# Seven half products in the last unit's output layer, TensorE transposes for the second unit, and a newly fitted order of steps

## The chip, the core and the metric

The kernel runs on one core of a Trainium2 chip. The metric is the device time in microseconds. A profiled execution was recorded as well: its trace gives the start and end of every instruction, and its "span" is the time from the first to the last of them.

## What is computed

The reference is a gated linear recurrence followed by a feed-forward block. The recurrence has 4 batches, 8 heads, 768 positions and a head size of 48.

```python
mag = np.sqrt(a_re * a_re + a_im * a_im)
scale = np.minimum(mag, 0.999) / (mag + 1e-06)
a_re_n, a_im_n = (a_re * scale, a_im * scale)
...
for t in range(S):
    new_re = ar * S_re - ai * S_im
    new_im = ar * S_im + ai * S_re
    S_re, S_im = (new_re + kv, new_im)          # kv: outer product of k[t] and v[t]
    y[:, :, t] = np.einsum('bhd,bhde->bhe', q[:, :, t], S_re)
...
h = x @ w_in                                    # x: y as 3072 x 384; w_in 384 x 2048
sp = np.maximum(h, 0.0) + np.log1p(np.exp(-np.abs(h)))
g = h * erf(sp)
return (g @ w_out).astype(np.float32)           # w_out 2048 x 384
```

## The kernel before

**Tiling.** The 3072 tokens are cut into 12 units of 256 tokens (three to a batch), each unit u into two chunks c of 128 tokens. The recurrence is done in chunks: running sums of the logarithms and angles of the gates, keys and queries scaled and turned by them, scores of a chunk with a triangular mask, and a state carried from chunk to chunk. The feed-forward block works on a whole unit: 2048 hidden columns in two slabs (`sl`) of 8 tiles, four steps of two tiles each.

**The order.** The Python program does not emit the work unit by unit. Every piece of work is a generator, called a step, and the string `ORDER` names the steps one after another; each mention advances that step to its next `yield` (the loop at the end of `quotient_path`). So the string fixes, word by word, the order in which each engine's in-order queue gets its instructions, and SyncE's (SP) queue its transfers. All instructions are there for the same work whatever the order; only the ACT table loads depend on it, since `act` (L780 to L786) emits one (L785) only where the next function belongs to another set than the last one (Ln and Exp; Arctan and Sin; Gelu). The names used below:

- `n0`..`n15` load a piece of the weights as 64-bit words and make float32 of it on VectorE (DVE, L843 to L848). `i0`..`i15` ("look") load a piece again and reduce it on DVE (L858). For i below 14 that load goes into the buffer that the slabs call `z` or `yy`, of which there is one each.
- `m t o l r a s p` with a unit number are the gates: ACT functions, DVE arithmetic, running sums on TensorE (PE).
- `k q v g` are loads. `K` and `Q` are `prep` (L1040, L1045): two DVE multiplications that write `kt` or `qt`. Keys and queries are then needed with the head dimension on the partitions, in a tile `KQ` (one buffer). **Unit 0** gets there by `kT` and `qT` (`turn`, L1069 and L1073): four PE transposes into PSUM and a copy out of it. **Units 1 to 11** get there by a DVE transpose of blocks (L1051, a third yield of `prep`) into a tile `X`, and by `M` (`move`, L1062): twelve transfers of 64 KB on SP's queue that put the blocks in their places.
- `A` are the scores (PE L1082, DVE L1086), `S` the state (PE L1101), `Y` the result (PE L1137, ACT copy L1139 into `xT`).
- `h` is `ff_in`: 6 matmuls (12 records in the trace, L1150) and an ACT copy (L1153); there are two PSUM buffers for it. `x` is `softplus`: four ACT functions over a whole slab, in the single buffers `z` and `yy`. `e` is `erf_times_h`: a Gelu on ACT into `e` (two buffers) and four DVE operations (L1178 to L1184), four parts to a slab. `z` is free for the next slab once its last L1180 has read it, `yy` once the last L1182 has.
- `O` is the output product. **Units 0 to 2 and unit 11** use `ff_out_8` (L1211): 16 steps of two matmuls with 384 columns (L1219), then an ACT scaling (L1226) and the store. **Units 3 to 10** use `ff_out_7` (L1241): the product is written as a 2x2 block product in half tiles, of which seven are computed instead of eight. Fourteen steps `O{u}.0` to `O{u}.13` of four matmuls with 192 columns each (L1254): a product for each slab, X, Y, Z and W being PSUM tiles. It needs sums of blocks of h: `f{u}.{sl}` (two DVE operations, L1195 and L1197), `sum_2` (L1265) once d (`O.1`, `O.2`) has read them, `read_x` (L1269) once b (`O.4`, `O.5`) has; and its PSUM tiles are brought out by DVE (L1262, L1274).
- The sums of the weights that the seven products use are made in place by `b0`..`b6` (L893), so the second half of `w_out_sb` in each first half slab is no longer there for unit 11. `d0` and `d1` (`restore`, L1238) put it back into a tile `B12`, and unit 11's `ff_out_8` takes two matmuls of 192 columns (L1221, L1222) for such a tile.
- `u` are matmuls whose result is not read. `Z` is `check`: DVE reductions, one PE product (L1326), DVE comparisons (L1330, L1331) whose result is read by all engines for a branch at the end.

Of the kernel before, what the change touches and what calls it, by code (L numbers as in the profile page):

```python
# [10 lines left out]
FP = mybir.dt.float32  # L11
# [9 lines left out]
P = 128  # L21
# [28 lines left out]
g0.0 u2_25 u2_41 u2_22 u4_2 u2_34 u4_38 u4_20 g0.0 u8_0 g0.1 g0.1 t0.0 m0.0 t0.0 t0.0 m0.0 m0.0 t0.1 l0.0 o0.0  # L50
t0.1 t0.1 l0.0 o0.1 l0.0 l0.0 l0.0 m0.1 m0.1 m0.1 l0.1 p0.0 p0.0 p0.0 u2_24 u8_1 n0 n0 n0 n0 n1 n1 n1 n1 r0.0
a0.0 n3 n3 a0.0 a0.0 a0.0 k0.0 u4_21 K0.0 n3 u2_23 r0.1 a0.1 a0.1 u2_40 q0.0 Q0.0 s0.0 s0.0 s0.0 K0.0 l0.1
kT0.0.1 Q0.0 qT0.0.0 qT0.0.1 a0.1 l0.1 l0.1 g1.0 t1.0 t1.0 qT0.0.0 a0.1 s0.1 l0.1 kT0.0.1 n3 g1.0 t1.0 v0.0 g1.1
t1.1 kT0.0.0 kT0.0.0 o1.0 p0.1 n2 n2 qT0.0.1 A0.0.1 A0.0.1 S0.0 g1.1 t1.1 p0.1 n2 p0.0 t1.1 k0.1 p0.1 K0.1 n2
r1.0 a1.0 a1.0 s0.1 s0.1 K0.1 m1.1 m1.1 m1.1 o1.1 v0.1 m1.0 a1.0 A0.0.0 p0.0 S0.0 a1.0 A0.0.0 n4 m1.0 m1.0 q0.1
Q0.1 n6 kT0.1.1 n4 p0.1 kT0.1.1 l1.1 l1.1 l1.0 l1.0 Q0.1 l1.1 S0.1 l1.0 l1.0 S0.1 l1.1 n4 Y0.0 kT0.1.0 kT0.1.0
l1.0 l1.1 n4 qT0.1.1 qT0.1.1 qT0.1.0 qT0.1.0 A0.1.1 A0.1.1 n5 p1.0 A0.1.0 A0.1.0 p0.1 S0.1 n5 q1.0 Y0.0 p1.0
Q1.0 p1.0 s1.0 s1.0 k1.0 K1.0 n5 r1.1 g2.1 s1.0 Q1.0 a1.1 K1.0 Q1.0 K1.0 Y0.1 Y0.1 p1.1 p1.1 a1.1 n5 a1.1 a1.1
q1.1 Q1.1 g2.0 m2 t2 t2 g2.0 g2.1 m2 h0.0.2 h0.0.2 m2 l2 l2 n6 s1.1 p1.1 t2 n6 l2 l2 o2 l2 n6 k1.1 h0.0.0 h0.0.0
p1.0 h0.0.4 v1.0 r2 n7 s1.1 s1.1 h0.0.6 h0.0.6 h0.0.4 x0.0 x0.0 e0.0.0 n7 l2 M1.0 M1.0 M1.0 M1.0 K1.1 l2 n7 Q1.1  # L60
n7 A1.0.0 A1.0.0 A1.0.1 A1.0.1 S1.0 n8 K1.1 a2.0 q2.0 p1.1 v1.1 k2.0 Q1.1 Y1.0 Y1.0 K1.1 p1.0 h0.1.6 n9 S1.0
M1.1 a2.0 M1.1 a2.0 a2.0 n8 e0.0.2 a2.0 a2.0 a2.0 a2.1 h0.1.6 p2.0 p2.0 p2.1 p2.1 p2.0 n8 n8 a2.1 n9 a2.1 a2.1
S1.0 Q2.0 h0.1.0 h0.1.0 p2.1 a2.1 a2.1 a2.1 s2 n9 n9 M1.1 M1.1 K2.0 S1.1 u2_39 A1.1.0 A1.1.0 A1.1.1 A1.1.1 g3.1
g3.0 s2 s2 K2.0 Q2.0 g3.0 S1.1 K2.0 g3.1 t3 t3 t3 m3 m3 p1.1 S1.1 o3 r3 Y1.1 Y1.1 a3.0 m3 l3 q2.1 h0.1.4 Q2.1
k2.1 Q2.0 h0.1.4 h0.1.2 v2.0 S2.0 p2.0 l3 h0.1.2 Q2.1 l3 K2.1 a3.0 a3.0 x0.0 K2.1 a3.0 x0.0 n10 n10 h1.1.0
h1.1.0 l3 h1.0.0 S2.0 l3 n10 l3 a3.0 l3 p3.0 p3.1 p3.1 p3.1 p2.0 p3.0 p3.0 h1.0.0 S2.0 h1.0.2 M2.0 M2.0 M2.0
e0.0.2 e0.0.0 M2.0 A2.0.1 A2.0.0 e0.0.2 e0.0.0 a3.1 a3.1 e0.0.2 e0.0.0 a3.1 a3.1 e0.0.0 e0.0.4 a3.1 A2.0.1
e0.0.2 a3.1 h1.0.2 e0.0.6 a3.1 s3 s3 s3 h1.0.6 g4.1 n11 g4.0 p3.0 g4.1 q3.0 h1.0.6 m4 k3.0 h1.0.4 h1.0.4 t4
A2.0.0 Y2.0 h1.1.6 K2.1 v2.1 g4.0 e0.0.4 t4 m4 n10 Q2.1 e0.0.4 e0.0.6 M2.1 M2.1 h1.1.2 e0.0.4 n11 e0.0.4 n11
e0.0.6 O0.1 Q3.0 K3.0 e0.0.6 m4 M2.1 M2.1 n12 p3.0 e0.0.6 K3.0 n11 x0.1 n13 v3.0 l4 x0.1 l4 l4 k3.1 t4 Q3.0 o4  # L70
l4 K3.0 l4 Y2.0 x0.1 O0.0 O0.2 O0.4 A2.1.1 A2.1.1 x0.1 l4 Q3.0 l4 a4.0 A2.1.0 A2.1.0 e0.1.0 e0.1.0 e0.1.2 e0.1.2
e0.1.0 e0.1.2 h1.1.6 e0.1.0 e0.1.2 e0.1.0 r4 a4.0 e0.1.2 e0.1.6 e0.1.6 a4.0 a4.0 O0.3 O0.5 O0.7 e0.1.4 e0.1.4
n12 Y2.1 Y2.1 e0.1.6 h1.1.4 h1.1.4 h1.1.2 e0.1.4 S3.0 n12 a4.0 a4.0 a4.0 q3.1 M3.0 M3.0 M3.0 n12 p3.1 M3.0
e0.1.6 e0.1.4 n13 K3.1 n13 S3.0 a4.1 a4.1 Q3.1 x1.0 x1.0 x1.0 a4.1 O0.6 h2.0.0 O0.8 O0.9 A3.0.0 n13 p4.0 p4.0
p4.1 p4.1 p4.1 p4.0 x1.0 h2.0.2 a4.1 K3.1 a4.1 O0.11 n15 v3.1 S3.1 O0.10 n15 e0.1.4 n15 e0.1.6 n15 e1.0.2 e1.0.2
e1.0.0 e1.0.0 e1.0.2 e1.0.0 e1.0.2 g5.1 e1.0.0 e1.0.2 e1.0.0 g5.0 g5.1 g5.0 p4.0 n14 h2.0.0 m5 a4.1 h2.0.2 m5 m5
n14 e1.0.6 e1.0.6 h2.0.6 h2.0.6 n14 e1.0.4 n14 e1.0.4 t5 e1.0.6 e1.0.4 e1.0.4 l5 Q3.1 t5 K3.1 e1.0.6 Q3.1 h2.1.0
h2.1.0 l5 x1.1 A3.0.1 A3.0.1 l5 l5 t5 l5 e1.0.4 x1.1 h2.1.2 h2.1.2 M3.1 M3.1 x1.1 M3.1 O0.12 O0.14 O0.13 O0.15
O0.15 h2.1.4 x1.1 h2.0.4 e1.0.6 a4.1 l5 A3.0.0 O1.0 O1.2 O1.4 o5 l5 e1.1.0 e1.1.0 e1.1.2 e1.1.2 e1.1.0 e1.1.0
e1.1.0 e1.1.2 s4 s4 r5 s4 e1.1.2 e1.1.2 q4.1 k4.0 K4.0 K4.0 e1.1.4 e1.1.4 e1.1.4 p3.1 M3.1 v4.1 e1.1.6 e1.1.6  # L80
h2.1.4 e1.1.6 e1.1.6 O1.6 Y3.0 O1.8 A3.1.1 A3.1.1 A3.1.0 A3.1.0 O0.15 v4.0 a5.0 q4.0 h2.1.6 O1.10 O0.14 O0.14
h2.0.4 x2.0 O1.1 S3.1 S3.1 Y3.1 Y3.0 S4.0 e1.1.4 x2.0 a5.0 a5.0 K4.0 k4.1 K4.1 x2.0 Q4.0 e1.1.4 Q4.0 Y3.1 Q4.0
e1.1.6 p4.1 M4.0 a5.0 K4.1 Q4.1 S4.0 x2.0 q5.1 M4.0 M4.0 M4.0 e2.0.0 e2.0.0 e2.0.0 h2.1.6 e2.0.2 e2.0.2 e2.0.0
e2.0.2 e2.0.0 e2.0.2 e2.0.2 O1.12 p5.0 p5.0 p5.0 h3.0.6 h3.0.6 O1.14 e2.0.6 e2.0.6 p5.1 O1.3 O1.5 a5.0 a5.0 a5.0
a5.1 e2.0.6 h3.0.2 e2.0.4 e2.0.4 e2.0.4 e2.0.4 O1.14 p5.1 p5.1 q5.0 x2.1 e2.0.4 a5.1 a5.1 e2.0.6 e2.0.6 x2.1
h3.0.2 x2.1 h3.0.0 h3.0.0 A4.0.0 O2.0 S4.1 Q4.1 a5.1 a5.1 A4.0.1 p4.0 S4.0 Q4.1 A4.0.0 S4.1 k5.0 O2.2 A4.0.1
Y4.0 v5.1 K5.0 K4.1 a5.1 a5.1 x2.1 e2.1.0 e2.1.0 e2.1.0 e2.1.2 e2.1.2 e2.1.2 e2.1.2 e2.1.0 s5 s5 e2.1.0 e2.1.2
s5 K5.0 p4.1 g6.0 g6.1 g6.1 e2.1.4 e2.1.4 O1.14 g6.0 e2.1.6 e2.1.6 e2.1.6 e2.1.6 e2.1.4 Y4.0 M4.1 v5.0 k5.1 S4.1
M4.1 M4.1 M4.1 m6 m6 h3.0.4 h3.0.4 x3.0 O1.7 O1.9 O1.11 O1.13 h3.1.4 O1.15 A4.1.1 S5.0 m6 l6 O1.15 t6 K5.0 Q5.0
Q5.0 Q5.0 l6 A4.1.0 A4.1.0 O2.1 x3.0 O2.3 A4.1.1 Y4.1 e2.1.4 l6 l6 e2.1.6 Q5.1 e2.1.4 Q5.1 v6.0 q6.0 l6 l6 x3.0  # L90
t6 t6 S5.0 h3.1.4 x3.0 o6 l6 K5.1 e3.0.2 e3.0.2 e3.0.0 e3.0.0 e3.0.2 e3.0.0 e3.0.2 e3.0.0 r6 e3.0.2 e3.0.0
h3.1.2 h3.1.2 a6.0 a6.0 e3.0.6 e3.0.6 O2.5 O2.7 O2.4 h3.1.6 e3.0.4 h3.1.6 e3.0.4 e3.0.6 e3.0.4 h3.1.0 h3.1.0
a6.0 a6.0 M5.0 a6.0 v6.1 M5.0 M5.0 M5.0 A5.0.0 a6.1 O1.15 p5.0 p5.0 A5.0.1 A5.0.1 A5.0.0 x3.1 O2.6 O2.9 O2.11
Y4.1 x3.1 Y5.0 e3.0.4 e3.0.6 K5.1 a6.1 a6.1 K5.1 x3.1 b6 a6.1 Q5.1 e3.0.6 M5.1 a6.1 a6.1 a6.1 b4 e3.0.4 Y5.0
f3.0 f3.0 x3.1 b0 S5.0 e3.1.2 e3.1.2 e3.1.0 s6 e3.1.2 e3.1.2 e3.1.0 e3.1.0 O2.13 e3.1.2 e3.1.0 e3.1.0 p6.1 p6.1
O2.8 p6.0 p6.0 Q6.0 e3.1.4 O2.15 h4.0.0 h4.0.0 e3.1.4 e3.1.4 e3.1.6 e3.1.6 e3.1.6 O2.10 O2.12 O2.14 g7.0 g7.1
g7.1 g7.0 M5.1 m7 M5.1 M5.1 m7 m7 b6 b2 e3.1.4 e3.1.6 e3.1.4 b4 b2 b0 b6 s6 s6 Q6.0 h4.0.2 h4.0.2 l7 O2.15 l7
h4.0.4 h4.0.4 i0 i0 h4.0.6 e3.1.6 f3.1 l7 h4.0.6 b0 b0 O2.14 l7 l7 k6.1 i1 x4.0 i1 t7 x4.0 t7 x4.0 p6.1 x4.0 b2
b2 b4 t7 A5.1.0 h4.1.6 O3.0 A5.1.0 A5.1.1 A5.1.1 l7 b4 l7 o7 p6.1 q6.1 O3.1 O3.2 O3.1 O3.2 e4.0.0 e4.0.0 e4.0.0
h4.1.6 e4.0.2 e4.0.2 e4.0.2 e4.0.0 e4.0.2 e4.0.0 e4.0.2 h4.1.0 h4.1.0 r7 b6 e4.0.6 e4.0.6 Y5.1 Y5.1 O3.3 e4.0.6  # L100
e4.0.4 e4.0.4 e4.0.4 Q6.0 f3.1 a7.0 e4.0.6 h4.1.4 h4.1.4 h4.1.2 h4.1.2 x4.1 O2.15 O2.14 e4.0.4 k6.0 p6.0 p6.0
p6.0 K6.0 a7.0 K6.0 O3.6 O3.4 O3.5 O3.5 O3.5 O3.4 O3.5 K6.0 M6.0 O3.7 h5.0.4 O3.7 e4.0.6 e4.0.4 M6.0 M6.0 x4.1
x4.1 a7.0 a7.0 Q6.1 O3.7 x4.1 K6.1 e4.1.2 e4.1.2 e4.1.0 e4.1.0 h5.0.2 e4.1.2 e4.1.0 e4.1.2 e4.1.2 p7.0 p7.0 p7.0
O3.8 a7.0 e4.1.0 e4.1.0 O3.9 O3.10 O3.11 O3.12 e4.1.6 e4.1.6 e4.1.6 h5.0.4 e4.1.4 e4.1.4 e4.1.4 e4.1.6 h5.0.2
a7.0 a7.0 e4.1.4 e4.1.4 p7.1 p7.1 M6.0 g8.0 p7.0 k7.0 f4.0 e4.1.6 i2 f4.1 a7.1 a7.1 O3.11 O3.13 O3.13 i2 a7.1
a7.1 f4.1 h5.0.0 h5.0.0 h5.0.6 h5.0.6 p7.1 x5.0 A6.0.0 A6.0.0 i3 i3 S6.0 S6.0 O4.1 O4.2 a7.1 a7.1 a7.1 O4.1 O4.2
p6.1 g8.1 x5.0 x5.0 O3.11 m8 O3.13 g8.0 g8.1 x5.0 Q6.1 Q6.1 f4.0 K6.1 K6.1 O4.0 O4.3 O4.4 A6.0.1 O4.5 O4.5
A6.0.1 O4.4 e5.0.0 e5.0.0 e5.0.0 e5.0.2 m8 m8 l8 e5.0.2 e5.0.0 e5.0.2 h5.1.4 h5.1.4 t8 l8 s7 l8 S6.1 e5.0.2
e5.0.0 e5.0.2 O4.5 l8 S6.1 O4.5 e5.0.4 e5.0.6 h5.1.0 h5.1.0 S6.1 l8 v7.1 p7.1 p7.0 M6.1 M6.1 q7.1 M6.1 M6.1
e5.0.4 e5.0.6 e5.0.4 O4.6 h5.1.2 O4.7 O4.7 e5.0.6 q7.0 K7.0 Q7.0 O4.7 e5.0.6 s7 s7 Q7.0 Y6.0 h5.1.2 K7.0 l8  # L110
e5.0.6 l8 e5.0.4 h5.1.6 h5.1.6 x5.1 t8 x5.1 Y6.0 x5.1 k7.1 v8.0 e5.0.4 A6.1.0 A6.1.0 t8 A6.1.1 A6.1.1 Q7.0 x5.1
K7.1 K7.0 O4.8 O4.9 O4.10 O4.11 v7.0 S7.0 e5.1.0 O4.12 Y6.1 Y6.1 S7.0 K7.1 o8 e5.1.0 e5.1.0 e5.1.2 e5.1.2 e5.1.0
# [569 lines left out]
def quotient_path(  # L682
# [27 lines left out]
    C = 2  # L710
# [722 lines left out]
```

## Time and profile before

| what | value |
|---|---|
| runs: median (lowest to highest of 3) | 674.85 us (671.51 to 676.1) |
| the profiled execution's own time | 671.15 us |
| its span | 669.4 us, 12235 instructions |
| last PE product of the output layer ends | 662.3 us |
| ACT table loads | 99, 127.0 us |
| `KQ` transfers | 264 of 64 KB |
| SP's queue, waiting for DVE's `X` | 76.1 us in 15 waits |
| mean granted PE clock | 0.996 |

In the profile, a group of instructions is given as line, engine, operation, "output<-input", then the count, the busy time in total and the mean of one in ns, and the engine's idle time just before. PE is TensorE's matmul, PEld its weight load, DVE VectorE, ACT ScalarE, SPq SyncE's queue of transfers. In the table by stretches each engine has its busy time and, in brackets, its number of instructions; then follow the clock granted to PE, the mean busy share of the 16 DMA engines and GB/s. In the timeline a row starts with start and length in us; the square bracket at the end is the idle time before it and what ended it.

### The profile page before, as it was taken

Reading aid. Unit: us, or ns where it says so; the run is one execution under the profiler, and the core shown is the slowest. Engines: PE = TensorE matmul, PEld = TensorE weight load, DVE = VectorE, ACT = ScalarE, POOL = GpSimd, SP = SyncE. Lnnn points to the kernel's source line nnn. Section 1 sums busy time; section 2 is a strip of 40 time slices with the busy share of each in tenths; the row PEclk is TensorE's granted clock in tenths of the full one; section 3 lists DMA queues with packets and bytes.
Section 4 is the critical chain, followed back from the end, with each engine's and each line's share of the span. In section 5 each row is a group of like instructions: output and inputs, shape, how many; then the busy total and the mean of one; then the engine's idle time right before and its main releaser. Section 6 shows DMA issues by size and latency. Waiting matters only on the chain.

```text
span 669.4 us, 12235 instructions
## 1 busy us (share of the span) xinstructions
PE 642.9 (96%) x4680; PEld 558.7 (83%) x4680; DVE 605.5 (90%) x984; ACT 581.5 (87%) x761; POOL 1.1 (0%) x8
## 2 busy tenths in 40 slices
PE   8788899999999999999999999999999999999995
PEld 7566787777677777999998999999998998999984
DVE  6999799999998999999999998999999898968844
ACT  6999889999999999996998997998998877676750
POOL 0000000000000000000000000000000000000000
PEclk9999899999999999999999999999999999999999
DMA  9877767762557328217526536625644534340000
GB/s 254 242 170 171 134 134 129 167 163 33 112 95 130 65 44 179 58 22 181 96 48 153 120 48 146 135 52 120 143 72 77 141 68 103 110 107 13 1 24 29
DMA packets 295468, 71.81 MB, mean 107 GB/s; under 512 B 282068, under 2 KB 285160, under 8 KB 295400
## 3 DMA queue, kind: packets, MB, share of 16 engines
q1 hardware_dynamic: 293320, 70.54, 49.5%
q8 instruction: 39, 0.64, 0.4%
q10 hardware_dynamic: 2080, 0.39, 0.3%
q14 instruction: 29, 0.24, 0.1%
HBM read 48.82 MB, written 4.75 MB: 80 GB/s over the span
## 4 chain that ended last, share of the span: by engine, by line
PE 39%; ACT 34%; DVE 16%; issue 4%; SPq 3%; DMA 3%; DVEq 0%; ACTq 0%
PE hps L1150 16%; ACT L785 7%; PE ops L1219 6%; ACT yy L786 6%; ACT z L786 5%; ACT CS L786 3%; PE sc L1082 3%; ACT e L786 3%; PE Z L1254 2%; PE X L1254 2%; SPq L1062 2%; PE y L1137 2%; DVE yy L1180 2%; ACT th L786 2%; DVE z L1178 2%
## 5 line engine op out<-in xcount | busy, mean ns | idle before, releaser
L1150 PE MATMUL hps<-xT,w_in_sb 128*128 128x256 f32 x1152 | 261.4, 381 | 1.5 <-ACT h L1153 1.3
L1150 PEld LDWEIGHTS hps<-xT,w_in_sb 128*128 128x128 f32 x1152 | 216.0, 190 | 34.5 <-ACT h L1153 4.3
L785 ACT ACT_TABLE_LOAD x99 | 127.0, 1283 | 3.7 <-issue 2.1
L1178 DVE TENSOR_TENSOR z<-z,yy 128x512 f32<-128x512 f32 x96 | 64.7, 687 | 23.0 <-ACT e L786 22.6
L786 ACT ACTIVATE e<-z 128x512 f32<-128x512 f32 x96 | 58.0, 628 | 22.8 <-DVE h L1184 22.2
L1219 PE MATMUL ops<-w_out_sb,h 128*128 128x384 f32 x224 | 77.3, 488 | 0.4 <-ACT out L1226 0.4
L1153 ACT COPY h<-hps 128x512 f32<-128x512 f32 x96 | 54.3, 577 | 14.8 <-PE hps L1150 14.8
L1180 DVE SCALAR_TENSOR_TENSOR yy<-z,yy 128x512 f32<-128x512 f32 x96 | 64.7, 688 | 1.7
L1184 DVE SCALAR_TENSOR_TENSOR h<-e,h 128x512 f32<-128x512 f32 x96 | 64.7, 685 | 1.2
L1182 DVE TENSOR_TENSOR e<-e,yy 128x512 f32<-128x512 f32 x96 | 64.6, 685 | 1.0
L1219 PEld LDWEIGHTS ops<-w_out_sb,h 128*128 128x128 f32 x224 | 41.6, 190 | 23.9 <-ACT out L1226 0.6
L1082 PEld LDWEIGHTS sc<-KQ 96*128 96x128 f32 x384 | 48.2, 194 | 9.7 <-issue 5.3
L1082 PE MATMUL sc<-KQ 96*128 96x128 f32 x384 | 50.3, 280 | 5.4 <-DMA KQ<-X 4.0
L786 ACT ACTIVATE z<-h 128x2048 f32<-128x2048 f32 x24 | 45.9, 1915 | 5.4 <-DVE seen L858 3.9
L786 ACT ACTIVATE yy<-z 128x2048 f32<-128x2048 f32 x24 | 45.9, 1913 | 2.1 <-DVE e L1182 1.8
L786 ACT ACTIVATE z<-z 128x2048 f32<-128x2048 f32 x24 | 45.8, 1910 | 0.4
L786 ACT ACTIVATE yy<-yy 128x2048 f32<-128x2048 f32 x24 | 45.9, 1914 | 0.3
L1086 DVE TENSOR_TENSOR A<-sc,triu 128x512 f32<-128x512 f32 x48 | 32.0, 681 | 3.4 <-PE sc L1082 3.4
L1137 PE MATMUL y<-A,v 128*32 128x128 f32 x768 | 33.7, 277 | 0.9 <-DVE A L1086 0.9
L1101 PEld LDWEIGHTS kv<-v,kt 128*96 128x96 f32 x320 | 29.7, 165 | 2.4 <-PE tr L1069 0.7
L1101 PE MATMUL kv<-v,kt 128*96 128x48 f32 x320 | 29.9, 246 | 0.5 <-PE tr L1069 0.5
L1137 PEld LDWEIGHTS y<-A,v 128*32 128x32 f32 x768 | 20.7, 110 | 8.0 <-issue 3.2
(119 smaller groups left out, 1043.2 us busy)
## 6 DMA issues: line engine op xcount, KB each, us to landing
KQ<-X SPq DMA_DIRECT2D x264, 64.0 KB
raw<-in_moe_w_in_dram SPq DMA_DIRECT2D x8, 768.0 KB
raw<-in_moe_w_out_dram SPq DMA_DIRECT2D x8, 768.0 KB
again<-in_moe_w_in_dram SPq DMA_DIRECT2D x8, 768.0 KB
ar<-in_a_re_dram SPq DMA_DIRECT2D x24, 192.0 KB
k<-in_k_dram SPq DMA_DIRECT2D x24, 192.0 KB
q<-in_q_dram SPq DMA_DIRECT2D x24, 192.0 KB
v<-in_v_dram SPq DMA_DIRECT2D x48, 96.0 KB
```

The lines of the kernel that those rows point to most:

```text
L785: scalar.preload_act_table_set(sets[0])
L786: scalar.activation(func=func, **kw)
L1082: nc.tensor.matmul(out=ps[:, j, :], lhsT=head("k", g * HG + j, u, c), rhs=head("q", g * HG + j, u, c), start=True, stop=True)
L1101: nc.tensor.matmul(out=kv[0:D2, j, :], lhsT=T["kt", u, c][:, j].rearrange("p u d -> p (u d)"), rhs=side(T["v", u][:, c, j // 2], j % 2), s ...
L1137: nc.tensor.matmul(out=ps[b * QUAD:(b + 1) * QUAD, i, :], lhsT=lhsT, rhs=rhs, start=start, stop=stop)
L1150: nc.tensor.matmul(out=ps[:, e, :], lhsT=w_in_sb[:, (sl * SLAB + i) // 2, kd, e * P:(e + 1) * P], rhs=T["xT", u][:, kd, :], start=(kd == 0 ...
L1153: scalar.copy(out=T["h", u, sl][:, i:i + 2, :], in_=ps)
L1178: vector.tensor_tensor(out=z, in0=z, in1=y, op=OP.mult)
L1180: vector.scalar_tensor_tensor(out=y, in0=z, scalar=-2.0, in1=y, op0=OP.add, op1=OP.mult)
L1182: vector.tensor_tensor(out=e, in0=e, in1=y, op=OP.mult)
L1184: vector.scalar_tensor_tensor(out=h, in0=e, scalar=1.0 / RT2, in1=h, op0=OP.add, op1=OP.mult)
L1219: nc.tensor.matmul(out=ps, lhsT=lhsT, rhs=w_out_sb[:, i, :], start=i == HALF, stop=i == KF - 1)
```

## The change

Three things are done.

1. `plain` loses `or u == NU - 1`: unit 11 uses `ff_out_7` and has `f11.0` and `f11.1`; `restore`, `B12`, `d0` and `d1` are gone.
2. `TURNS = 2`: units 0 and 1 use `turn`, units 2 to 11 `move`. In `turn` only the keys of unit 0's chunk 0 are copied by DVE, all others by ACT. `prep` of unit 1 has two yields.
3. `ORDER` is another string: 2303 words against 2291. Beside the words that 1 and 2 add and remove it has the same words, nearly all in other places. Read off the two strings, ACT changes its table set 99 times before and 94 times after.

`g_angle` takes the place of the previous chunk's angles later than before, in a function of its own; what it emits is the same.

```diff
+    TURNS = 2
...
-        prev = None
+        prev = lambda: T["F", u][:, c - 1, :] if c > 0 else T["F", u - 1][:, C - 1, :]
...
-        if u > 0:
+        if u >= TURNS:
             x = whole(att1, "X", (u, c), [P, D2 // QUAD, 2 * H, QUAD])
...
-        (vector.tensor_copy if nm == "k" and c == 0 else scalar.copy)(out=columns(u, c)[0:D2, i:i + HG], in_=ps[0:D2])
+        (vector.tensor_copy if nm == "k" and u == 0 and c == 0 else scalar.copy)(out=columns(u, c)[0:D2, i:i + HG], in_=ps[0:D2])
...
-                if u < PLAIN or e >= HALF:
-                    nc.tensor.matmul(out=ps, lhsT=lhsT, rhs=w_out_sb[:, i, :], start=i == HALF, stop=i == KF - 1)
-                else:
-                    nc.tensor.matmul(out=ps[:, :HD], lhsT=lhsT, rhs=w_out_sb[:, i, :HD], start=False, stop=False)
-                    nc.tensor.matmul(out=ps[:, HD:], lhsT=lhsT, rhs=T["B12"][:, sl * HALF + e], start=False, stop=False)
+                nc.tensor.matmul(out=ps, lhsT=lhsT, rhs=w_out_sb[:, i, :], start=i == HALF, stop=i == KF - 1)
...
-    def restore(sl):
...
-    for sl in range(NSL):
-        steps[f"d{sl}"] = restore(sl)
     for u in range(NU):
-        plain = u < PLAIN or u == NU - 1
+        plain = u < PLAIN
...
-            if u > 0:
+            if u >= TURNS:
                 steps["M" + at] = move(u, c)
```

The end of the new order, from the last unit's first softplus on (a name that recurs is the same step going on):

```diff
+e10.1.2 f10.1 f10.1 h11.0.2 x11.0 x11.0 x11.0 x11.0 e11.0.4 e11.0.4 e11.0.4 h11.1.6 e11.0.0 e11.0.0 e11.0.4
+e11.0.0 e11.0.4 e11.0.0 e11.0.0 h11.1.2 h11.1.2 e11.0.2 e11.0.2 e11.0.6 e11.0.2 e11.0.6 e11.0.6 e11.0.2 e11.0.2
+e11.0.6 O10.1 h11.1.0 O10.1 h11.1.0 h11.1.4 h11.1.4 x11.1 x11.1 x11.1 x11.1 e11.1.2 O10.2 O10.2 e11.0.6 O10.0
+O10.3 O10.4 O10.6 O10.5 e11.1.0 O10.5 O10.7 O10.5 O10.5 O10.7 O10.7 O10.8 O10.9 O10.4 O10.10 e11.1.2 e11.1.0
+e11.1.2 e11.1.0 e11.1.2 e11.1.0 O10.11 e11.1.2 e11.1.0 f11.0 O10.11 O10.11 O10.12 O10.13 e11.1.4 e11.1.4 e11.1.6
+e11.1.6 e11.1.4 O10.13 e11.1.6 e11.1.4 e11.1.6 e11.1.4 e11.1.6 f11.1 f11.1 O11.0 O10.13 O11.1 O11.3 O11.1 O11.2
+O11.2 f11.0 O11.4 O11.5 O11.5 O11.4 O11.6 O11.5 O11.5 O11.7 O11.7 O11.12 O11.7 O11.8 O11.9 O11.10 O11.11 O11.13
+O11.11 O11.11 Z Z O11.13 O11.13 Z
```

## The prediction

> **What bounds the kernel now.** I read the page's shares first. Three engines are nearly full, so a share alone doesn't tell which one sets the time.
>
> ```profile
> PE 642.9 (96%) x4680; PEld 558.7 (83%) x4680; DVE 605.5 (90%) x984; ACT 581.5 (87%) x761; POOL 1.1 (0%) x8
> ```
>
> Then the table by stretches. PE is all but gapless from 98 us on (511.1 of 515 us, then 49.5 up to its last product at 662.3), and it is the only engine that is; what it lacks, it lacks ahead of 98 us.
>
> ```profile
> 0.00:98.00 98.00, 82.41 (x662) 68.52 (x663) 85.60 (x144) 87.30 (x150) 1.09 (x8) 0.98 0.80 181
> 98.00:613.00 515.00, 511.08 (x3762) 446.71 (x3761) 486.00 (x774) 465.11 (x580) 0.00 (x0) 1.00 0.50 103
> 613.00:670.00 57.00, 49.46 (x259) 43.51 (x257) 33.92 (x68) 29.12 (x31) 0.00 (x0) 0.98 0.05 16
> ```
>
> To turn this into a sum I price PE's steps at the pace that they keep back to back in the chain of waits: `h` 2.59 us, a step of the plain product 1.29, one of the seven 1.30, scores 0.90, `Y` 1.90 (0.95 without a state), `S` 1.33, a group of four transposes 0.44 (eight took 1.08, of which I take 0.2 for latency). 96 x 2.59 + 64 x 1.29 + 112 x 1.30 + 48 x 0.90 + 41.8 + 26.6 + 8 x 0.44 + 27.3 (running sums) + 10.6 (unread and check) = 629.8 us. The last product ends at 662.3, so PE idles 32.5 us. Taking the work that the order puts ahead of each of the 24 `Y` from the time at which it starts shows where: 10.9 us lost by `Y0.0`, 22.7 by `Y1.1` (78.7 us), 24.7 by `Y2.0` (105.9 us), then only 7.7 more up to the end. **The time is PE's work, plus 25 us lost at the start, plus 8, plus 7.1 us from PE's last product to the end of the span.**
>
> In the start two waits on transfers stand out, and SP's queue, 9.4, 4.4 and 4.0 us long:
>
> ```profile
> PE sc L1082 <- DMA KQ<-X: 2.9, 2, 1.6
> ```
> ```profile
> 46.12 9.38 SPq L1062 DMA_DIRECT2D KQ<-X  x12
> 63.79 4.35 SPq L1062 DMA_DIRECT2D KQ<-X  x6
> 68.85 3.97 SPq L1062 DMA_DIRECT2D KQ<-X  x6
> ```
>
> At the end, the rows of ACT and DVE show a second chain just as late as PE: the slabs' single `z` and `yy` buffers. Softplus starts at 592.23, 614.94 and 634.49, and the last h is written at 658.39, when PE has just the three steps left that need it.
>
> ```profile
> 614.94 1.91 ACT L786 ACTIVATE z<-h 128x2048 f32<-128x2048 f32 x1
> 634.49 1.92 ACT L786 ACTIVATE z<-h 128x2048 f32<-128x2048 f32 x1 [0.57 <-DVE yy L1180]
> ```
> ```profile
> 657.71 0.68 DVE L1184 SCALAR_TENSOR_TENSOR h<-e,h 128x512 f32<-128x512 f32 x1
> 658.30 4.03 PE L1219 MATMUL ops<-w_out_sb,h 128*128 128x384 f32 x12
> ```
>
> **What the Trainium skill says.** "Perfetto Trace Analysis", Identifying the Most-Contended Engine: PE's busy share is no measure of headroom. The trace agrees: 82.4 us busy in the first 98, for some 73 us of work. "VectorE: DVE Perf Modes", The three transpose paths: DVE transposes 32x32 blocks only, TensorE the full 128x128 into PSUM. That is why `move` needs twelve transfers; the trace has them. "TensorE: Matmul & The Clock Gate", Part 4: a PE transpose needs a copy out of PSUM and takes about 275 ns in a kernel; here 278, but 0.11 us each in a row. "ScalarE: Activation LUTs", What ACT_TABLE_LOAD costs: 1283 ns and a drain of 1380. The 99 loads took 1283 each, but the row after a load starts 0.02 us later and the one before ends 0.02 us earlier, so I count 1.28.
>
> **The change, part by part.**
>
> *Seven products in unit 11.* PE: 16 x 1.29 = 20.6 us go, 14 x 1.30 = 18.2 come: -2.4. DVE: `d0`, `d1` (2 x 0.95) go; four `f` operations, four of `sum_2` and `read_x` at 0.68 and 2.5 us of bringing out come: +6.0. ACT loses two scalings (1.0). But DVE and ACT have slack here (33.9 and 29.1 busy of 57), and the dependence is what counts. Now three steps (3.9 us) follow the last h. In the new order eleven products follow: `f11.1` writes the sum that `O11.2` needs, and `O11.2` and all behind it (5, 4, 6, 7, 12, 8 to 11, 13) come after, 11 x 1.30 = 14.3 us. The waits among them (`sum_2` before `O11.5`, `read_x` before `O11.11`) are covered by the products between.
>
> So the last chain, laid out with measured times, from the end of `h11.0.2` on PE = 0: copy and table load, first softplus at 2.0; four functions, two accumulator reads and a table load 9.2 (614.94 to 624.52 is 9.6 with a copy), Gelu and hand-over 0.67: DVE starts at 11.9. Twelve operations to the last L1180, about 0.62 each with the later Gelus hidden: 19.7; table load after two copies: second softplus at 20.0 (18.0 behind the first; now 19.6, with 1.6 us of restore and bringing out in between). Again 9.9: DVE at 29.9; eight operations, `f11.0`, `read_z`, eight operations, `read_w`, first of `f11.1`: 41.7. PE's work to `O11.2` is `O9` 5.2, `h11.1` 10.4, `O10` 18.2, `O11.0`, `.1`, `.3` 3.9: 37.7, and 0.8 for a copy that frees a PSUM buffer. **PE waits 0.8 + 3.2 = 4.0 us where it waits for nothing now.** PE's end is at 56.0 after `h11.0.2`.
>
> *Transposes in unit 1.* PE +8 x 0.44 = 3.5 us. ACT +8 copies of 0.57 = 4.6, in the stretch where it is busy 87.3 of 98. DVE -4 x 0.97 = 3.9. SP loses 24 issues of 64 KB: 9.4 + 4.4 + 4.0 = 17.7 us of its queue, and whatever stands behind them (w, gates, q, k, v of unit 2) goes out earlier; now the q load is issued at 78.46, DVE gets on at 81.20, and ACT waits 1.6 us at 84.83. The new wait: transposes share two PSUM buffers with the scores, so `kT1.1.1` stands in PE's queue until ACT has copied `qT1.1.0` (61.0 us of ACT work, so some 71 us), with `A1.1`, `h0.1.4` and `Y1.1` behind it; now the same scores stand until 75.9 for the transfer. PE work is -2.4 + 3.5 = +1.1: 630.9 us.
>
> *The order.* Five table loads fewer: 6.4 us of ACT. ACT isn't the bound after 98 us, so by itself worth nothing; it makes room for the copies. In the start I add up ACT's and PE's work ahead of the same points. In the new order PE's last wait of size is `h1.0.0` for the copy of `Y1.1`, with 74.7 us of ACT work ahead. The same copy now starts at 85.6 with 71.6 done, so ACT had idled 14.0; without the 1.6 above, 12.4. It lands at 87.5, when PE has had 68.0 us of work: idle 19.5 against 23.4 now at the corresponding place (81.29), because `h0.1.6` and `h0.1.0` now stand between the scores and the result, where nothing waits for a transfer. I add 0.5 for small waits behind it: **20.0 in place of 24.8**. Bounds: 16 if ACT's idle falls to 9, 24.8 if the copies eat it. The rest of the order (98 us to the last unit) I put at the same 7.7: DVE's and ACT's sums ahead of each slab differ from the old ones by -12 to +10 us, PE's queue is gapless now and can only lose; bounds 6 to 11.
>
> **Sum**, against the profiled span of 669.4: 630.9 + 20.0 + 7.7 + 4.0 = 662.6 for PE's end, + 7.1 for the check, + 0.35 as `read_w` stands ahead of the comparisons on DVE: 670.1, that is +0.7. The execution's own time was 671.15; the median of the runs, 674.85, is 3.7 above it, and I carry the difference over to it: 675.5.
>
> **Rivals.**
>
> *Faster.* The order's start leaves ACT only 9 us idle (PE 16) and the last chain isn't waited for (0 in place of 4.0): 670.1 - 4.0 - 4.0 = 662.1, median 667.5. For it: all three engines' loads in the start are no larger, SP's is far smaller. Against it: softplus of `x11.0` can't start before `h11.0` is through PE, and the 41.7 us behind it are durations, not slack.
>
> *The copies take it back.* ACT is what the start runs on; 4.6 us more of it and PE idles 24.8 as now: +4.8, 674.9, median 680.3. For it: ACT busy 89%. Against it: the ACT work ahead of `h1.0.0` and `h1.0.4` is 2.2 and 2.9 us lower in the new order, copies included.
>
> *Slower: the last chain starts late.* If `x11.0` starts when it does now, 614.94, in place of 608.4 (606.4 for PE plus 2.0), `O11.2` comes at 614.94 + 39.7 = 654.6 and PE ends at 668.9: span 676.4, median 681.9. Each us beyond 608.4 goes into the end whole; slower by over 1% is from 614.5 on. For it: between the slabs, `i12` and `i13` load into `z` and `yy`, and softplus waited 3.6 us for them at 572.55; the sums of ACT and DVE work ahead of `x11.0` are only 2.6 and 0.2 us lower. Against it: five DVE operations of unit 10 now stand ahead of `x11.0` that don't hold its buffer.
>
> That the change doesn't do what it says is excluded by the order's text: `O11.0` to `O11.13` and `f11` are in it, `M1` isn't.
>
> **How the numbers follow.** Mine 0.43, copies 0.19, faster 0.20, slower 0.18. A difference of 1% is about what a measurement of this kernel can tell from none. Mine and the copies' lie within 1% of 674.85 (668.1 to 681.6): 0.62. Cases of both signs lie outside, 667 to 683 holds eight in ten; my own case alone is 671 to 679.
>
> **What would show it.** Right: PE's work ahead of `Y2.0` against its start gives about 20 us; no wait on KQ before 70 us; softplus `x11.0` near 608; PE idle 3 to 4 us at the second slab's first product with S; the last product 14 us after the last h. Wrong: an idle of PE under 17 or over 24 at 100 us, idle PE of over 3 us between 110 and 600, or `x11.0` waiting for DVE.

## The result, and the profile after

Median of 22 runs each: 674.7 us after, 672.7 us before, ratio 1.0028, 95% interval 1.0012 to 1.0045. The change costs 0.3%. The prediction held 1% to be about what a measurement can tell from none; with 22 runs of each kernel 0.3% can be told. The profiled execution has a span of 672.3 us (before 669.4).

The busy shares of the changed kernel, then its stretches (length, busy time and instructions of PE, PEld, DVE, ACT, POOL, clock, DMA, GB/s):

```profile
PE 646.0 (96%) x4728; PEld 562.2 (84%) x4728; DVE 609.6 (91%) x992; ACT 578.7 (86%) x762; POOL 1.1 (0%) x8
```
```profile
0.00:98.00 98.00, 89.18 (x746) 76.26 (x750) 88.35 (x150) 92.01 (x163) 1.08 (x8) 1.00 0.78 187
98.00:616.00 518.00, 510.54 (x3728) 442.93 (x3721) 485.05 (x768) 466.00 (x578) 0.00 (x0) 1.00 0.48 98
616.00:673.00 57.00, 46.26 (x264) 43.00 (x262) 36.16 (x76) 20.65 (x24) 0.00 (x0) 0.97 0.06 20
```

PE is 6.8 us busier in the first 98 us, and its clock there is 1.00 in place of 0.98: the start is better. In the middle stretch it lacks 7.5 us of 518, where it lacked 3.9 of 515: the middle is worse. The end in the timeline (start, length), on ACT and then on PE:

```profile
610.37 1.91 ACT L787 ACTIVATE z<-h 128x2048 f32<-128x2048 f32 x1
628.36 1.91 ACT L787 ACTIVATE z<-h 128x2048 f32<-128x2048 f32 x1
```
```profile
650.09 1.57 PE L1244 MATMUL Y<-T,S 128*128 128x192 f32 x8 [0.87 <-DVE S L1197]
...
663.29 1.46 PE L1244 MATMUL W<-w_out_sb,h 128*128 128x192 f32 x8
664.76 0.19 PE L1316 MATMUL all<-sums,column 128*1 128x6 f32 x2
```

Softplus `x11.0` starts 4.6 us earlier than before, yet PE's last product ends 2.5 us later (664.8 against 662.3).

The prediction's own measure shows how much PE has idled up to a given `Y`: the work that the order puts ahead of this `Y` on PE is subtracted from the time at which the `Y` starts. What is left is idle time, in us (work at half clock counts in it too):

| up to | before | after | forecast |
|---|---|---|---|
| Y1.1 | 22.7 | 14.2 | |
| Y2.0 | 24.7 | 15.3 | 20.0 |
| Y4.0 | 26.5 | 19.0 | |
| Y6.0 | 29.2 | 23.9 | |
| Y8.0 | 29.7 | 26.1 | |
| Y11.1 | 32.3 | 29.4 | 27.7 |
| last product | 32.5 | 33.9 | 31.7 |

Up to Y2.0 (the start) 9.4 us are gained. From there to Y11.1 (the middle) 6.5 of them are lost again, behind it (the end) 4.3, and there are 1.1 us more work. The first question: is PE's lead only waited away in the middle, because a chain of work on ACT and DVE (90% and 94% busy there) sets the pace (**theory 1**), or is the new middle worse by itself (**theory 2**)? The second: what do the parts do alone?

### The profile page after: what moved, and what is told of

Same layout as the page of the kernel before. It is cut to its first block, busy times and chain, and to the rows that moved or that the text cites. A ratio compares the mean times of both kernels' runs of the same rounds, so it can differ in the third digit from the quotient of the medians.

```text
span 672.3 us, 12307 instructions
## 1 busy us (share of the span) xinstructions
PE 646.0 (96%) x4728; PEld 562.2 (84%) x4728; DVE 609.6 (91%) x992; ACT 578.7 (86%) x762; POOL 1.1 (0%) x8
## 4 chain that ended last, share of the span: by engine, by line
ACT 41%; PE 24%; DVE 23%; issue 4%; DMA 4%; SPq 2%; POOL 0%; DVEq 0%; ACTq 0%; POOLq 0%
PE hps L1152 10%; ACT L786 10%; ACT z L787 7%; ACT yy L787 6%; ACT e L787 3%; DVE yy L1182 3%; DVE z L1180 3%; PE Y L1244 3%; DVE e L1184 2%; ACT h L1155 2%; ACT CS L787 2%; DVE h L1186 2%; PE X L1244 2%; ACT y L787 2%; ACT pr L787 2%
## 5 line engine op out<-in xcount | busy, mean ns | idle before, releaser
L787 ACT ACTIVATE e<-z 128x512 f32<-128x512 f32 x96 | 57.8, 627 | 24.7 <-DVE h L1186 23.9
L1220 PE MATMUL ops<-w_out_sb,h 128*128 128x384 f32 x192 | 66.1, 487 | 0.0
L1220 PEld LDWEIGHTS ops<-w_out_sb,h 128*128 128x128 f32 x192 | 35.6, 190 | 20.2 <-DVE h L1186 0.6
```

The lines of the kernel that those rows point to most:

```text
L787: scalar.activation(func=func, **kw)
L1220: nc.tensor.matmul(out=ps, lhsT=lhsT, rhs=w_out_sb[:, i, :], start=i == HALF, stop=i == KF - 1)
```

## The experiments

All ratios are to runs of the kernel before on the same chip. Because the two orders name the same steps, a start of one can be joined to the rest of the other: the rest is taken in its own sequence, without the mentions already made. In the cuts below "..." stands for words left out.

**Starts, middles and ends exchanged.** e1 has the new start, and the old middle and end:

```diff
 the new order's words 1 to 501: ... h1.1.4 h1.1.6 Y2.0 r4 e0.1.0 e0.1.0 e0.1.0
-the rest of the new order
+the rest of the old one: v2.1 h1.1.2 a4.0 ... (last unit plain, with d0, d1)
```

> The first 501 words of the new order (up to the second mention of Y2.0 and the first steps behind it), then the rest of the old order; unit 1 on TensorE transposes, the last unit plain as before. PE's work is 629.8 + 3.5 = 633.3 us. Theory 1 (the middle is paced by the chain of slabs on ACT and DVE, so PE's lead is only waited away, whatever the order): PE has idled 15.3 us at Y2.0, but 28 to 31 at Y11.1; end of PE 662 to 665, span 669 to 672, ratio to before 0.999 to 1.004. Theory 2 (the new order's middle is worse by itself): the old middle adds its old 7.6, idle 23 at Y11.1, end of PE 656.5, span 663.6, ratio 0.991.

e2 has the new start and middle, and the old end:

```diff
 the new order's words 1 to 2143: ... Y11.1 O9.7 Y11.1 x10.1
-the rest of the new order
+the rest of the old one: i14 O9.8 O9.9 O9.10 ... (last unit plain, with d0, d1)
```

> The new order up to its Y11.1, then the old order's rest; unit 1 on TensorE transposes, the last unit plain with its restore. That is the change without the seven products of unit 11. PE's work 633.3 us, idle at Y11.1 as after (29.4), and hardly any behind it, since the last slab's chain (43.5 us from softplus x11.0 at 610.4 to the last h, 653.9) leaves PE's last work at about 663: end of PE 663, span 670, ratio to before 1.001, which is 2.3 us (0.35%) under after. If the chain at the end bounds the plain form as well, the last h is later than 656 and the span 672 or more.

e3 has the old start, e4 the old start and middle, both with unit 1 on the transfers and the new end:

```diff
-the new order's start
+the old order's words 1 to 521 (e3: ... M3.0 e0.1.6 e0.1.4) or 1 to 2147 (e4: ... A11.1.0 Y11.1 Y11.1)
 the rest of the new one (seven products in unit 11)
```

> The old order's first 521 words, then the rest of the new one; unit 1 on the transfers as before, the last unit by seven products. PE's work 627.4 us. Theory 1: PE comes to the middle with 24.7 us idled and gains on the slabs' chain what it gained before: idle at Y11.1 30 to 33, wait at the end 4.2, end of PE 662 to 665, span 669.5 to 672.5, ratio 1.000 to 1.005. Theory 2: the new middle costs its 14.1 here too, idle 38.8, span 677.9, ratio 1.013.

> The old order up to Y11.1, then the new one's rest: the kernel before with nothing but seven products in unit 11. PE's work 627.4 us, idle at Y11.1 as before, 32.3. If softplus x11.0 starts as soon as h11.0 is through PE (about 608.5): the wait at O11.2 is 4.2, end of PE 664, span 671.5, ratio 1.003. If it stays at 614.9, where it was before: O11.2 at 654.6, end of PE 669.3, span 676.8, ratio 1.011.

| kernel | start | middle | end | span | idle at Y2.0, Y11.1 | ratio (95% interval) |
|---|---|---|---|---|---|---|
| before | old | old | plain | 669.4 | 24.7, 32.3 | 1 |
| e1 | new | old | plain | 665.3 | 15.3, 24.7 | 0.9942 (0.9917 to 0.9966) |
| e2 | new | new | plain | 669.1 | 14.5, 28.6 | 0.9983 (0.9969 to 0.9997) |
| after | new | new | seven | 672.3 | 15.3, 29.4 | 1.0028 (1.0012 to 1.0045) |
| e3 | old | new | seven | 679.8 | 25.4, 40.6 | 1.0166 (1.0130 to 1.0201) |
| e4 | old | old | seven | 677.1 | 25.3, 31.8 | 1.0130 (1.0096 to 1.0165) |

Read the first four lines as a ladder: the new start with its transposes gains 0.6%, the new middle loses 0.4%, and the seven products with the order of their end lose 0.45%. Theory 1 falls on both sides. In e1 the old middle adds 9.4 us of idling to the new start, where it adds 7.6 in the kernel before (2.4 of the 9.4 fall between Y2.1 and Y3.0, right behind the join), so most of the lead is kept; in e3 the new middle adds 15.2 to an old start, where there is no lead to wait away (4.9 of them at the join). Counted from Y3.0 to Y11.1, behind both joins, PE idles 6.6 us in the kernel before and 5.0 in e1, but 11.3 in the changed kernel and 10.0 in e3. The words of the middle decide, whatever the start was: theory 2 holds.

In e4 I had expected `x11.0` at 608.5 or at 614.9. It started at 613.81, as soon as `h11.0` was through PE. e4's row on ACT, and two rows on PE:

```profile
613.81 1.91 ACT L786 ACTIVATE z<-h 128x2048 f32<-128x2048 f32 x1
...
655.00 1.57 PE L1243 MATMUL Y<-T,S 128*128 128x192 f32 x8 [0.86 <-DVE S L1196]
...
669.68 0.19 PE L1315 MATMUL all<-sums,column 128*1 128x6 f32 x2
```

The same rows of e2:

```profile
614.76 1.91 ACT L786 ACTIVATE z<-h 128x2048 f32<-128x2048 f32 x1
...
662.08 0.20 PE L1325 MATMUL all<-sums,column 128*1 128x6 f32 x2
```

From the start of `x11.0` to the end of the last product it is 55.9 us in e4 (with PE at half clock for 3.4 us of them, from 624.8 on) and 54.4 in the changed kernel. With the plain product it is 47.3 in e2, in e1 and in the kernel before. So in these orders seven products need `x11.0` about 7 us earlier to break even. The new end brings it 4.4 earlier than e2's, which has the same start and middle, and the missing 2.7 is what PE's end loses (664.76 against 662.08).

**What makes the new middle worse: the looks?** In the middle of the changed kernel, DVE waits for loads of the looks, in the kernel before it doesn't. DVE's waits from 98 to 600 us (total us, times, longest), after:

```profile
DVE z L1180 <- ACT e L787: 9.8, 13, 2.3
DVE seen L859 <- DMA again<-in_moe_w_out_dram: 4.5, 3, 3.3
...
DVE seen L859 <- DMA again<-in_moe_w_in_dram: 1.0, 2, 0.8
```

e5 is the kernel after, e6 the kernel before, each with

```diff
-i0 i0 i1 i1 ... i13 i13 (all mentions)
```

> The changed kernel without the looks i0 to i13 (left out: that part of the check of the weights; the first value of the checked numbers stays, the output is the same). 14 loads of 512 KB and 14 reductions of 0.87 us on DVE go. Theory A (in the new middle the looks are what DVE, and behind it PE, waits for: 5.5 us of DVE waiting for these loads, none before): PE's idle from Y2.0 to Y11.1 falls from 14.1 to 9 or less, span 667 or less, ratio to before 0.996 or less. Theory B (the many small waits come from where the words stand, the looks are no cause): idle 12 to 14, span 670 to 672, ratio 1.000 to 1.003.

> The kernel before without the looks i0 to i13 (left out as in e5). Theory A: DVE waits for none of these loads here, so little is gained, span 668 to 669.4, ratio 0.998 to 1.000; softplus at 572.55, which waited 3.6 us for one, starts earlier without use for PE. Theory B: the gain is as large or small as in e5.

e5 has a span of 669.4 us and a ratio of 0.9973 (0.9952 to 0.9994); PE idles 11.9 us from Y2.0 to Y11.1, against 14.1 with the looks. e6 has a ratio of 0.9960 (0.9937 to 0.9982), and PE idles 5.2 us in the middle, against 7.6. (The span of e6's profiled execution is longer, 671.1, because it lost 4.0 us more in the start, at a clock of 0.82 from 20 to 40 us.) Both kernels gain alike, 2.2 and 2.4 us in the middle, 0.55% and 0.40% in the runs. The looks cost both; they aren't the difference. So the theory that the looks make the new middle worse (A in the expectations) falls, though DVE's wait for them is in plain sight.

**The parts of the start.** e7 is the kernel before with only the transposes, e8 is e1 with the transfers:

```diff
-M1.0 M1.0 M1.0 M1.0
+qT1.0.0 kT1.0.0 qT1.0.0 kT1.0.0 qT1.0.1 kT1.0.1 qT1.0.1 kT1.0.1
...
-M1.1 ... M1.1 ... M1.1 M1.1
+qT1.1.0 kT1.1.0 ... qT1.1.0 kT1.1.0 ... qT1.1.1 kT1.1.1 qT1.1.1 kT1.1.1
```
```diff
-qT1.0.0 ... (and all other qT1 and kT1)
+M1.0 M1.0 M1.0 M1.0 (where qT1.0.0 first stood; M1.1 likewise)
```

> The kernel before with nothing but the transposes for unit 1: its words stand where the transfers M1.0 and M1.1 stood. PE +3.5 us of work, SP -17.7 us of queue. If the transfers themselves cost the start: no wait for KQ there, the loads of unit 2 earlier, PE's idle at Y2.0 falls from 24.7 to about 18 to 20, span 666 to 668, ratio 0.995 to 0.998. If it is the order of the start: idle stays at 24 to 25, span 672 to 673, ratio 1.004 to 1.006.

> e1 with unit 1 on the transfers again (at the places of the first transpose of each chunk), so the new order of the start without the transposes; old order behind it, last unit plain. PE's work 629.8. If the order alone makes the start: idle at Y2.0 15 to 16, at Y11.1 25, span 662, ratio 0.989. If it needs the transposes: PE waits for KQ again, idle at Y2.0 20 or more, span 667 or more, ratio 0.996 or more.

Both are far slower than either forecast. e7 has a ratio of 1.0201 (1.0140 to 1.0263), and PE has idled 40.8 us at Y2.0; e8 has 1.0152 (1.0099 to 1.0205) and 33.5 us. The largest waits of PE between 40 and 130 us in e7, then in e8:

```profile
PE tr L1068 <- ACT KQ L1072: 8.0, 1, 8.0
```
```profile
PE sc L1081 <- DMA KQ<-X: 9.4, 3, 7.5
```

In e7 the copy that frees the transposes' buffer stands in ACT's queue behind the first two functions of `x0.0`, a Gelu and two table loads:

```profile
58.83 1.91 ACT L786 ACTIVATE z<-h 128x2048 f32<-128x2048 f32 x1
...
62.79 1.28 ACT L785 ACT_TABLE_LOAD   x1
64.08 0.63 ACT L786 ACTIVATE e<-z 128x512 f32<-128x512 f32 x1
64.62 1.05 ACT L1072 COPY KQ<-tr 96x512 f32<-96x512 f32 x2
```

In the old order a transfer covered this time; in the new order the copies (67.8 and 69.2 us) have no such block ahead of them, and PE waits 0.41 us for one. In e8 it is the scores that stand for 7.5 us until the transfers have landed. Each of the two parts, put alone where the other's words had stood, loses; the runs show only this placing of each, not the best one.

**The clock.** Part of the start's gain is the clock granted to PE. Two stretches of the kernel before, then the changed kernel:

```profile
72.00:76.00 4.00, 2.40 (x22) 2.06 (x23) 3.55 (x6) 3.18 (x6) 0.00 (x0) 1.00 0.48 76
76.00:80.00 4.00, 4.00 (x40) 3.69 (x44) 1.84 (x3) 3.94 (x5) 0.00 (x0) 0.59 1.03 183
```
```profile
60.00:80.00 20.00, 18.61 (x219) 15.62 (x218) 19.73 (x30) 19.86 (x34) 0.00 (x0) 1.00 0.76 189
```

Behind a stretch with PE 60% busy the clock is at half for 3.3 us of 4 (worked out from the 0.59), which is 1.6 us lost. In all seven profiles with the whole new start it is 1.00 from 40 to 98 us (in one it falls before that, 0.91 from 20 to 40); in the five with the whole old one it falls to 0.83 to 0.93 in one 20 us stretch or more between 40 and 100 us.

The single runs show how much hangs on this. In the 35 runs of the kernel before beside e1, the mean clock of a run lies between 0.979 and 0.998 and its span between 678.1 and 668.1 us; a straight line through them falls by about 5 us for each 0.01 of clock. The 22 runs of e2 on the same chip lie between 0.994 and 0.999, the 22 of the changed kernel between 0.993 and 0.998. Read off such lines at a clock of 0.997, the spans are 668.7 us before, 666.5 in e1, 669.8 in e2 and 672.6 after (estimates from these runs; the chip of the changed kernel's isn't known). So at an equal clock the start gains 2.2 us, where the medians of the times say 3.4, and the change as a whole costs about 4 us, of which its steadier clock hides half.

e10 tried to fill the gap in the kernel before:

```diff
-u2_39 A1.1.0
+u9_39 A1.1.0
```

> The kernel before with 9 unread products in place of 2 at u2_39, ahead of the scores of A1.1, where PE waits 1.6 us for KQ; nothing else. In the kernel before the clock granted to PE falls to about half in the 3.3 us behind that wait (0.59 in the stretch 76 to 80 us), and it doesn't in the changed kernel. If the wait is what lowers it: the stretch behind stays at 1.00, PE's idle at Y1.1 falls from 22.7 to 21 to 21.5 and at Y2.0 by as much, span 667.7 to 668.5, ratio 0.998. If the clock falls for another reason, or 1.5 us more of unread work delays the scores: idle by Y2.0 24.7 or more, ratio 1.000 to 1.002.

The ratio is 1.0005 (0.9983 to 1.0027), and PE has idled about 27 us at Y2.0. That is inconclusive. The profiled execution was a long one (678.0 us, where the median of e10's runs is 673.1), and in it the clock had already fallen at 73.3 us, behind an earlier wait of 1.76 us, so the unread products ran at half speed:

```profile
76.19 4.13 PE L1312 MATMUL unread<-ident 128*128 128x128 f32 x18
```

**Are the middle's waits real losses?** e12, the changed kernel with PE held up near 252 and 285 us:

```diff
-        for e in range(2):
+        for e in [0, 1] * (2 if u == 4 and i == 0 else 1):
```

> The changed kernel with the matmuls of h4.0.0 and h4.1.0 done twice (same result): PE is held up by 2 x 2.59 = 5.2 us, near 252 and near 285 us, nothing else is changed. If PE sets the pace of the new middle and its waits are each a loss: the waits behind stay as they were, the end moves by all 5.2, span 677 to 678, ratio to before 1.009 to 1.011. If PE there is ahead of ACT and DVE (what is left of theory 1): the waits behind 290 us, 7 us of idle up to Y11.1 in the changed kernel, take in half or more of it, span 673 to 675, ratio 1.003 to 1.007.

The ratio is 1.0104 (1.0078 to 1.0131), the span 676.3 us. Counted from Y2.0 on, 4.8 of the 5.2 us reach the end. The waits behind stay: PE's longest between 290 and 600 us is that of an output product for DVE's h, 1.1 us (0.9 in the changed kernel). So PE sets the pace there, and a delay of PE isn't made up later. e9 tries to mend three of PE's waits:

```diff
-O0.7 A2.1.1 t4 A2.1.0 O0.2 A2.1.1
+O0.7 t4 O0.2 A2.1.1 A2.1.0 A2.1.1
...
-A5.0.0 Y5.0 a6.1 a6.1 a6.1 O2.13 O2.15
+A5.0.0 a6.1 a6.1 a6.1 O2.13 Y5.0 O2.15
...
-O4.6 O4.0 O4.3
+O4.0 O4.3 O4.6
```

> The changed kernel with four words moved: the first mentions of A2.1.1 and A2.1.0 behind O0.2 (PE waited 0.84 us there for KQ), of Y5.0 behind O2.13 (1.03 us for DVE's mask), O4.6 behind O4.3 (0.87 us for DVE's h). If the new middle's loss is made of such local waits (theory B): each goes into the end, PE's idle from Y2.0 to Y11.1 falls from 14.1 to 11 to 11.7, span 669.5 to 670, ratio to before 0.999. If PE is only ahead of a chain on ACT and DVE that sets the pace (what is left of theory 1), the three waits come back as others: idle 13 to 14, span 671.5 to 672.5, ratio 1.002 to 1.004.

The ratio is 1.0013 (0.9992 to 1.0033), the span 670.6 us. PE idles 13.0 us in the middle, against 14.1: of the 2.7 us of the three waits 1.1 are regained. The runs alone don't tell e9 from the changed kernel. The first and third wait are gone. The second only moved to the next PE instruction, because DVE itself was late. The changed kernel, then e9:

```profile
245.20 0.42 PE L1139 MATMUL y<-A,v 128*32 128x128 f32 x8 [1.03 <-DVE A L1088]
```
```profile
244.48 0.44 PE L915 MATMUL sum<-parts,triu_r 128*128 128x384 f32 x1 [1.01 <-DVE parts L987]
```

**A better version.** e1 with its join mended. The waits there, in e1:

```profile
120.90 2.86 PE L1149 MATMUL hps<-xT,w_in_sb 128*128 128x256 f32 x12 [1.17 <-ACT h L1152]
...
135.23 1.13 PE L1081 MATMUL sc<-KQ 96*128 96x128 f32 x8 [2.20 <-DMA KQ<-X]
```

```diff
-v2.1 h1.1.2 a4.0 a4.0 ... Y2.1 Y2.1
+v2.1 a4.0 a4.0 ... Y2.1 h1.1.2 Y2.1
...
-O0.8 O0.9 A3.0.0 n13 ... S3.1 O0.10
+O0.8 O0.9 n13 ... S3.1 O0.10 A3.0.0
```

> e1 with two words moved at its seam: the first mention of A3.0.0 behind O0.10 (PE waited 2.2 us for KQ), of h1.1.2 behind the first Y2.1 (1.17 us for the copy of h). If such waits go into the end: idle at Y3.0 19.6 falls to 16.5, span 665.3 falls to 662 to 663, ratio to before 0.988 to 0.991. If the last slabs' chain (last h at 654 in e1, the last three steps of PE right behind it) now bounds the end: span 664 to 665.3, ratio 0.993.

The ratio is 0.9919 (0.9891 to 0.9947), the median 667.2 us, the span 663.7: e11 is faster than both kernels. Its interval overlaps with e1's, so the runs don't show that the two moved words help. PE has idled 14.3 us at Y2.0, 17.8 at Y3.0 and 23.1 at Y11.1. The idle time at Y3.0 is 1.3 us above the figure of the first forecast, and the span 0.7 above its range. In place of the two waits another one appeared, and behind it PE ran at half clock for 3.4 us, as the second row shows (2.86 us for twelve such matmuls above, 4.44 here):

```profile
126.20 0.44 PE L911 MATMUL sum<-parts,triu_r 128*128 128x384 f32 x1 [1.49 <-ACT xT L1138]
...
126.65 4.44 PE L1149 MATMUL hps<-xT,w_in_sb 128*128 128x256 f32 x12
```

A part of e11's gain is clock as well: at 0.997, such lines give 665.6 us for e11 and 668.3 for the kernel before beside it, 2.7 us of the 5.1 between the medians.

## Why the prediction held, and where its steps were wrong

675.5 was forecast and 674.7 measured, but that this is so close is luck, twice over. The forecast stood on a median of three runs of the kernel before, 674.85; over 22 runs it is 672.7. As a difference, 0.7 us were forecast and 2.0 measured; as a span, 670.1 was forecast and 672.3 measured. And the 2.2 us by which the span missed are what errors of opposite sign left over: the forecast put 4.7 us too much idle time of PE into the start, 6.4 too little into the middle and 0.5 too little into the end.

- *Seven products in unit 11: right.* From `x11.0` to `O11.2` 39.7 us were forecast and 39.7 measured; PE's waits behind `h11.0` 4.0 and about 4.2; from `O11.2` to PE's end 14.3 and 14.7. That this part costs more than its 2.4 us of saved work is shown by e2, whose span is 3.2 us shorter with the plain product. The 608.4 for `x11.0` (608.6 by the prediction's own sum, 662.6 less 56.0 and 2.0 more) was 610.4, because PE itself was later.
- *Copies and order in the start: wrong in size.* "ACT had idled 14.0; without the 1.6 above, 12.4" was the step that failed. Y1.1's copy started at 82.00 with 74.2 us of ACT work ahead of it, so ACT had idled 7.8 us. PE's idle at Y2.0 was 15.3, not 20.0, and outside the bound of 16. I had taken off only the one wait that I saw, and carried the old idle over for the rest; but the transfers and the order had shaped that too. The gaps between ACT's rows ahead of the same copy add up to 10.6 us in the kernel before, 5.4 in the changed kernel and 22.4 in e8, which has the new start with the transfers. I also read the clock of 0.98 in the table of stretches and gave it no term: 1.6 us. "TensorE: Matmul & The Clock Gate", Part 1, of the Trainium skill says that the default is a throttled clock and that idling brings it back; it names a whole idle window of about 3.4 us and, for one kernel, short idle times that come often. Here PE was 53% busy in the 3.4 us before the fall, and its longest wait there was 1.6 us. So no whole idle window was needed.
- *The rest of the order at the same 7.7: wrong.* It was 14.1, outside the bounds of 6 to 11. I reasoned that sums of ACT and DVE work differ little, so waits would too. Sums over slabs don't see a mask or an angle that stands a few instructions too late. Two of the forecast's three signs of being wrong appeared: PE's idle was under 17 us at 100 us, and it was over 3 us between 110 and 600 us, where the table above has some 13 (the forecast's own 7.7 would have shown this sign too). e1, e3 and e12 show that the loss belongs to the new middle and isn't a lead waited away; e5 and e6 show that it isn't the looks. Three waits of PE (2.7 us) were found and 1.1 us regained. Which words make up the rest stays open.
- *The rivals.* "The copies take it back" didn't happen (idle at Y2.0 fell by 9.4 us). "Faster" had the start right and the end wrong. "Slower: the last chain starts late" is what e4 is: `x11.0` started at 613.8 and PE ended at 669.7, where 614.9 and 668.9 were forecast. In the changed kernel `x11.0` started 3.4 us earlier than in e4.
- *From PE's end to the end of the span: right,* 7.45 forecast and 7.5 measured.

## What to carry to other kernels

A new order is a change in every stage: take its gain stage by stage, as work ahead of a mark against that mark's time, and exchange starts, middles and ends between the two orders before judging it as one, since here a gain of 0.6% lay hidden under two losses. Compare the clock of the runs as well as their times: it made up part of what looked like the gain of an order. A form of the last product with less work isn't cheaper when more of it has to stand behind the last result: compare the time from that result's first cause to the end (47.3 against 54.4 us), not the work. When an engine is late, moving the waiting word on another engine helps only if the next one doesn't wait for the same engine.

## What the runs showed of the hardware

The traces record when the clock granted to PE changes. In all 14 of them, every stretch at half clock ahead of PE's end lasts 3.41 us or a whole multiple of it (6.83, 13.65 and 17.07 occur), and the stretches at full clock between them are whole multiples too. Cut into these windows of 3.41 us, the traces show PE busy for 67% or less of the window before each fall; every window under 49% was followed by half clock, and those from 49% to 67% went either way. So the length of one wait doesn't decide. e11's wait of 1.49 us lay in one window, 56% busy, and half clock followed; e1's of 2.20 us lay across two, 73% and 62% busy, and the clock stayed.

In e7 a wait of 7.97 us brought half clock from 61.2 to 78.2 us. PE worked again from 65.2 us on, so by the clock alone the wait cost some 6.5 us more (half of these 13 us). Two of the windows, from 68.0 to 74.8 us, were busy throughout and were still followed by half clock; what besides busy time counts isn't shown here.

```profile
65.23 1.09 PE L1068 MATMUL tr<-ident,qt 128*96 128x128 f32 x4 [7.97 <-ACT KQ L1072]
66.12 1.06 PE L1068 MATMUL tr<-ident,kt 128*96 128x128 f32 x4
67.00 3.78 PE L1081 MATMUL sc<-KQ 96*128 96x128 f32 x16
```

The same four transposes took 0.60 us ahead of the wait and 1.09 behind it, and these scores 3.78 us against 2.05 in the changed kernel.
